# Fused pooled attention and feed-forward kernel: the first batch's loads, transposes and values rearranged, and the first tile's down stage taken by weight piece over four output banks

## The chip, the cores and the metric

One core of one Trainium2 chip runs the whole program. The metric is the device time of one execution in microseconds (us). The kernel before takes 303.81 us (median of 4 executions, 303.62 to 308.21). The span of the trace, from the first to the last instruction, is about 1.8 us shorter than the device time.

## The reference

```python
# q, k, v: (8 batches, 8 heads, 576 positions, 64); w_in (512, 2048); w_out (2048, 512)
k_p = k.reshape(B, H, 72, 8, D).mean(axis=3)          # v_p likewise
attn = softmax(q @ k_p.T / sqrt(D))                   # 576 x 72 per head
x = (attn @ v_p).transpose(0, 2, 1, 3).reshape(4608, 512)
h = x @ w_in
out = (h * cos(h)) @ w_out                            # 4608 x 512, float32
```

## The kernel before

Tokens are worked in nine tiles of 512. A tile has an **up stage** (64 matmuls `x @ w_in` in eight groups; each group fills a pair of PSUM banks, ScalarE takes the cosine of the pair and VectorE multiplies into `g_sb`) and a **down stage** (64 matmuls `g @ w_out`). The attention of the next batch is put between the down matmuls as a list of fills. It is worked in **units**, each a part of a batch's heads and positions: score matmuls, an exp on ScalarE, sums of the exps and their inverse, a **value block** (matmuls of the exps with pooled v) and a VectorE multiply by the inverse into `xT`, the input of the up stage. k and v are pooled by matmuls too. Before tile 0 there is nothing to overlap with, so batch 0's attention is a startup of its own.

The kernel uses eight banks of PSUM, the memory that matmuls write: three pairs (`banks`) and two single output banks (`obanks`). The parts that the change and the argument touch (cut):

```python
banks  = [psum.tile([128, 2, 512], FP32, name=f"bank{i}") for i in range(3)]
obanks = [psum.tile([128, 512], FP32, name=f"obank{i}") for i in range(2)]
msb = ctx.enter_context(tc.tile_pool(name="msb", bufs=3))      # output buffers o_sb: three
...
def up_g(t, fp, between=()):
    h = banks[fp % 3]
    nc.scalar.activation(out=cos, in_=h, func=ACTF.Sin, bias=half_pi[:, :1])
    ...
    nc.vector.tensor_mul(out=g_sb[:, 2 * fp:2 * fp + 2, :], in0=h, in1=cos)

def down_out(t, ms, ps, ...):            # one output chunk: PSUM to o_sb, then two DMAs
    o = msb.tile([128, d_model], FP32, name="o_sb", tag="o_sb")
    nc.vector.tensor_copy(out=o[:, 0:n], in_=ps)
    ...
# startup of batch 0
warm_up(10, obanks[0])                                   # matmuls on constants
pool_k_mm(0, obanks[1], 0, 2)(vec)
warm_up(2, banks[1][:, 0, :])
...                                                      # 9 transposes of q
warm_up(2, banks[1][:, 0, :])
scores(0, us[0], banks[0]); scores(0, us[1], banks[1])   # first exp: time E
...
sums_first(0, us[2], obanks[0])
values_then(0, us[0], obanks[1]); values_then(0, us[1], banks[1][:, 0, :])
sums_first(0, us[3], banks[2][:, 0, :])
values_then(0, us[2], obanks[1]); values_then(0, us[3], obanks[0])
up_mm(0, 0, 0, 2); up_mm(0, 1, 0, 2)                     # first half of 16 up matmuls
...
# tile 0's down stage: two output chunks at a time, batch 1's units between
mms = [(ms, fc) for hm in range(2) for cg in range(4) for ms in range(2 * hm, 2 * hm + 2)
       for fc in range(4 * cg, 4 * cg + 4)]
fill[1:] = [(2, S_(0, 0)), (8, lambda: pool_v_mm(1, banks[1])), ..., (13, V_(0, 1)), ..., (40, V_(3, 0))]
```

Times that the whole text uses, as the prediction names them: **E**, the first exp of batch 0; **R**, when the up matmuls over input chunks 2 and 3 resume (the ninth up matmul); **F**, the first down matmul of tile 0; **T1**, tile 1's first up matmul. The **tail** is T1 to the end of the span. **D** is when TensorE has finished all up-stage work of tile 0 and could start F.

The softmax here doesn't subtract the row's maximum and nothing guards it: scores larger than these inputs give would overflow.

## Time and profile before

| kernel before, profiled execution | us |
|---|---|
| span | 302.1 |
| E / R | 9.25 / 18.98 |
| F (no wait before it) | 33.50 |
| T1 | 53.50 |
| tail | 248.6 |

From T1 on TensorE's up and down matmuls follow each other without gaps in this trace, so the times before T1 are what a change of the startup can move. Besides the lines that the prediction shows, two things will matter later. The first is how TensorE passes the first microseconds (timeline: start, us, engine, line, operation, what is written and read, tile, count):

```profile
1.47 4.45 PE L391 MATMUL obank<-warm 128*128 128x512 bf16 x10 [1.47 <-DVE warm L336]
...
6.84 0.60 PE L391 MATMUL bank<-warm 128*128 128x512 bf16 x2
...
7.78 0.59 PE L391 MATMUL bank<-warm 128*128 128x512 bf16 x2
...
8.80 0.63 PE L211 MATMUL bank<-qT,kk 64*72 64x256 bf16 x8 [0.43 <-DVE qT L193]
```

The first ten matmuls have no use but to keep the array busy; two more follow twice, where TensorE would have waited. Ten take 4.45 us, some 0.43 us for 512 columns. The later pairs take 0.60 and 0.59 us; a matmul's end lies 0.38 us after its start when the clock is full, so their spacing is 0.21 to 0.22 us. The array runs at half speed first and at full speed by 6.84 us; the trace's clock records begin with full clock at 6.51 us.

The second is the load rate in 4 to 6 us (busy time by windows: width of the window, busy us and instructions of PE, its weight loads, VectorE, ScalarE and GpSimd, then granted clock, DMA share and GB/s):

```profile
4.00:6.00 2.00, 2.00 (x11) 0.60 (x11) 1.81 (x3) 1.15 (x1) 1.93 (x5) 1.00 0.97 132
```

The rate counts bytes as they are written. GpSimd's loads turn fp32 into bf16, so 132 GB/s written are 264 GB/s read.

### The profile page before, as it was taken

The numbers are of one execution on the slowest core, as the hardware profiler recorded it, in microseconds if no ns is written. First come the engines' busy times: TensorE is split into PE (matmuls) and PEld (weight loads), VectorE is DVE, ScalarE is ACT, GpSimd is POOL, SyncE is SP. The second block draws the span as 40 slices with busy tenths as digits, with TensorE's granted clock in tenths as the row PEclk, the third lists the DMA queues.
The fourth block names the chain that finished last, engine by engine and source line by source line (L and its number), as shares of the span: only waits on it lengthen the run. The fifth ranks groups of instructions, "written<-read, shape, count | busy, mean of one in ns | idle before, by whom it ended". The sixth has DMA issues, their size and how long they took to land.

```text
span 302.1 us, 4605 instructions
## 1 busy us (share of the span) xinstructions
PE 294.0 (97%) x1798; PEld 141.6 (47%) x1798; DVE 172.3 (57%) x211; ACT 206.8 (68%) x255; POOL 129.8 (43%) x92
## 2 busy tenths in 40 slices
PE   8799999999999999999999999999999999999995
PEld 3545544445544454455444544454444544444444
DVE  5558636574566366645675566656574567425712
ACT  3887897469856986688768876788578956606500
POOL 8553007984973596349733991399100000000000
PEclk9999999999999999999999999999999999999999
DMA  7999999639546943695169617881900330131032
GB/s 152 201 207 206 208 204 196 152 44 174 109 113 105 167 92 70 123 171 113 44 132 161 115 36 162 129 141 36 167 5 1 71 69 0 27 79 35 0 71 71
DMA packets 44006, 32.92 MB, mean 109 GB/s; under 512 B 22096, under 2 KB 39248, under 8 KB 43984
## 3 DMA queue, kind: packets, MB, share of 16 engines
q0 software_dynamic: 19744, 18.07, 38.2%
q1 hardware_dynamic: 24080, 14.42, 21.0%
q8 instruction: 14, 0.23, 0.3%
q10 hardware_dynamic: 160, 0.13, 0.2%
q14 instruction: 8, 0.07, 0.1%
HBM read 36.70 MB, written 9.44 MB: 153 GB/s over the span
## 4 chain that ended last, share of the span: by engine, by line
PE 85%; DMA 10%; POOL 2%; ACT 1%; issue 0%; DVE 0%; POOLq 0%; ACTq 0%
PE obank L310 39%; PE bank L297 37%; DMA w_out_sb<-in_moe_w_out_dram 6%; PE bank L241 5%; DMA w_in_sb<-in_moe_w_in_dram 4%; PE bank L211 3%; PE bank L328 1%; POOL kv_st L84 1%; POOL kp L384 1%; POOL q_b L84 1%; ACT L285 0%; ACT cos L304 0%; ACT ex L218 0%; POOL identity masks.py:197 0%; DVE o_sb L316 0%
## 5 line engine op out<-in xcount | busy, mean ns | idle before, releaser
L310 PE MATMUL obank<-w_out_sb,g_sb 128*128 128x512 bf16 x560 | 132.5, 380 | 0.5 <-DMA w_out_sb<-in_moe_w_out_dram 0.5
L297 PE MATMUL bank<-xT,w_in_sb 128*128 128x512 bf16 x576 | 126.5, 379 | 0.0
L304 ACT ACTIVATE cos<-bank,half_pi 128x1024 f32<-128x1024 f32 x72 | 80.0, 1113 | 63.3 <-PE bank L297 63.3
L307 DVE TENSOR_TENSOR g_sb<-bank,cos 128x1024 bf16<-128x1024 f32 x72 | 88.1, 1225 | 48.2 <-ACT cos L304 48.2
L297 PEld LDWEIGHTS <-w_in_sb 128*128 128x128 bf16 x576 | 55.5, 98 | 68.6 <-DVE xT L252 2.5
L310 PEld LDWEIGHTS <-g_sb 128*128 128x128 bf16 x560 | 52.2, 97 | 56.9 <-issue 3.7
L252 DVE TENSOR_TENSOR xT<-bank,inv 64x512 bf16<-64x512 f32 (+1 forms) x72 | 45.3, 629 | 50.1 <-ACT inv L248 49.2
L141 POOL TENSOR_TENSOR kv_st<-kv_st 72x2048 f32<-72x2048 bf16 x12 | 48.7, 4056 | 35.2 <-DMA kv_st<-in_k_dram 35.2
L247 ACT ACTIVATE lnc<-bank 64x512 f32<-64x512 f32 (+1 forms) x72 | 39.2, 544 | 2.9 <-PE bank L241 1.3
L218 ACT ACTIVATE ex<-bank 72x1024 bf16<-72x1024 f32 (+1 forms) x40 | 35.0, 928 | 5.3 <-PE bank L211 5.2
L316 DVE COPY o_sb<-obank 128x512 f32<-128x512 f32 x35 | 23.6, 689 | 16.8 <-PE obank L310 16.2
L142 POOL TENSOR_TENSOR kv_st<-kv_st 72x1024 f32<-72x1024 f32 x12 | 28.2, 2348 | 1.0
L248 ACT ACTIVATE inv<-lnc 128x512 f32<-128x512 f32 (+1 forms) x36 | 21.0, 583 | 1.1
L241 PE MATMUL bank<-ex,vz 72*128 72x256 bf16 (+1 forms) x176 | 20.0, 243 | 0.2 <-ACT ex L218 0.2
L241 PEld LDWEIGHTS <-vz 72*128 72x128 bf16 x176 | 13.7, 97 | 9.9 <-issue 0.6
L145 POOL TENSOR_TENSOR kp<-kv_st 72x512 bf16<-72x512 f32 x12 | 14.9, 1264 | 0.5
L211 PE MATMUL bank<-qT,kk 64*72 64x256 bf16 (+1 forms) x192 | 13.3, 252 | 1.1 <-ACT qT L193 0.5
L211 PEld LDWEIGHTS <-kk 64*72 64x72 bf16 x192 | 7.6, 110 | 11.9 <-issue 8.1
L285 ACT ACT_TABLE_LOAD x9 | 11.5, 1283 | 0.9 <-PEq L515 0.7
L288 ACT ACT_TABLE_LOAD x9 | 11.5, 1283 | 0.2
L495 POOL COPY gate<-kk 1x1 bf16<-1x1 bf16 x5 | 0.9, 180 | 24.7 <-DMA kk<-kp 24.7
L84 POOL DMA_DIRECT2D q_b<-in_q_dram x10 | 7.7, 773 | 2.7 <-DMA w_in_sb<-in_moe_w_in_dram 1.4
(55 smaller groups left out, 89.8 us busy)
## 6 DMA issues: line engine op xcount, KB each, us to landing
out_dram<-o_sb SPq DMA_DIRECT2D x70, 128.0 KB, 2.4
kv_st<-in_v_dram POOLq DMA_DIRECT2D x8, 576.0 KB, 13.0
kv_st<-in_k_dram POOLq DMA_DIRECT2D x7, 576.0 KB, 7.7
q_b<-in_q_dram POOLq DMA_DIRECT2D x6, 576.0 KB, 9.9
w_in_sb<-in_moe_w_in_dram POOLq DMA_DIRECT2D x4, 512.0 KB, 13.7
w_out_sb<-in_moe_w_out_dram POOLq DMA_DIRECT2D x4, 512.0 KB, 18.4
q_b<-in_q_dram POOLq DMA_DIRECT2D x4, 288.0 KB, 12.1
g_sb<-in_k_dram SPq DMA_DIRECT2D x1, 576.0 KB, 3.5
```

The source lines that it names most:

```text
L141: add(out=s, in0=x[:, :, 0:4, :], in1=x[:, :, 4:8, :], op=ADD)
L142: add(out=s[:, :, 0:2, :], in0=s[:, :, 0:2, :], in1=s[:, :, 2:4, :], op=ADD)
L211: nc.tensor.matmul(pair[:Sp, bank, c:c + n].rearrange("p (g n) -> p g n", n=64), lhsT=kk[b % 2][half[r], h0 + i, 0:Sp], rhs=att["qT", b][h ...
L218: nc.scalar.activation(out=ex[:, 0:nh * n].rearrange("p (a n) -> p a n", a=2), in_=pair[:Sp, :, 0:nh * n // 2], func=ACTF.Exp, scale=scale ...
L241: nc.tensor.matmul(pair[:, hp, (i // 2) * n:(i // 2 + 1) * n], lhsT=vz[b % 2][:, pj, 2 * hp:2 * hp + 2, :].rearrange("p a d -> p (a d)"), ...
L247: nc.scalar.activation(out=lnc[half[1 - hp]], in_=pair[half[1 - hp], hp, 0:w], func=ACTF.Ln)
L252: nc.vector.tensor_mul(out=x_out(b, u, half[hp]), in0=cols(pair[half[hp], hp, :], u), in1=cols(inv[half[1 - hp]], u))
L297: nc.tensor.matmul(h[:, j, :], lhsT=w_in_sb[fc // 4][:, ki, (fc % 4) * 128:(fc % 4 + 1) * 128], rhs=xT[:, ki, t * TILE:(t + 1) * TILE], st ...
L304: nc.scalar.activation(out=cos, in_=h, func=ACTF.Sin, bias=half_pi[:, :1])
L307: nc.vector.tensor_mul(out=g_sb[:, 2 * fp:2 * fp + 2, :], in0=h, in1=cos)
L310: nc.tensor.matmul(o, lhsT=g_sb[:, fc, ms * 128:(ms + 1) * 128], rhs=w_out_sb[fc // 4][:, fc % 4, :], start=(fc == 0), stop=(fc == FFCH - 1))
L316: nc.vector.tensor_copy(out=o[:, 0:n], in_=ps)
```

## The change

It has two parts.

1. **Startup of batch 0.** Half of q comes in fp32 over SyncE's queue behind k's half and is cast on VectorE; v comes in two loads. Pooled k, transposes, sums and values go to other banks, so that ScalarE has one copy less. v is pooled in two halves, the second after the first values; four up matmuls come before the values of units 2 and 3. Seven warm-up matmuls instead of ten, and the two later pairs are gone.
2. **Tile 0's down stage.** The weight pieces are gone through once, each for all four output chunks, so that a late piece of `w_out` is not waited for. Four chunks need four output banks: two halves of pair 2. Batch 1's units then share pairs 0 and 1, and the up groups of tile 0 are rotated by one pair. Batch 1's first pooling of k and its transposes of q run one up group later.

The core of the diff (cut; the new form of `pool_k_mm` and `pool_v_mm` and the moved mask code are left out):

```diff
-    def up_mm ...  h = banks[fp % 3]
+    def h_bank(t, fp):
+        return banks[(fp + (t == 0)) % 3]
...
-    load_even(staged["q", 0], 0, q, 0, 2)
+    for i, (which, src) in enumerate((("k", k), ("q", q))):
+        ...
+        nc.sync.dma_start(out=first[which], in_=even_view(src, 0, 0, 2))
...
-    warm_up(10, obanks[0])
-    pool_k_mm(0, obanks[1], 0, 2)(vec)
-    warm_up(2, banks[1][:, 0, :])
+    warm_up(7, obanks[0])
+    puts = pool_k_mm(0, obanks, 0, 2)
+    cast_first("q", vec)
+    puts[0](act)
+    puts[1](vec)
...
-    warm_up(2, banks[1][:, 0, :])
...
-    pool_v_mm(0, banks[1])
+    pool_v_mm(0, (banks[1][:, 0, :], banks[1][:, 1, :]), 0, 2)
     sums_first(0, us[2], obanks[0])
-    values_then(0, us[0], obanks[1])
-    values_then(0, us[1], banks[1][:, 0, :])
-    sums_first(0, us[3], banks[2][:, 0, :])
-    values_then(0, us[2], obanks[1])
-    values_then(0, us[3], obanks[0])
+    values_then(0, us[0], banks[0][:, 0, :])
+    values_then(0, us[1], banks[0][:, 1, :])
+    pool_v_mm(0, (banks[1][:, 0, :], banks[1][:, 1, :]), 2, 4)
+    sums_first(0, us[3], obanks[1])
     up_mm(0, 0, 0, 2)
+    values_then(0, us[2], obanks[0])
+    values_then(0, us[3], obanks[1])
     up_mm(0, 1, 0, 2)
...
+        ob = [obanks[ms % 2] for ms in range(4)]
         if t == 0:
-            mms = [(ms, fc) for hm in range(2) for cg in range(4) for ms in range(2 * hm, 2 * hm + 2) ...]
+            mms = [(ms, fc) for cg in range(4) for ms in (2, 3, 0, 1) for fc in range(4 * cg, 4 * cg + 4)]
+            ob[2:] = [banks[2][:, i, :] for i in range(2)]
...
-            fill[1:] = [(2, S_(0, 0)), (8, lambda: pool_v_mm(1, banks[1])), ..., (13, V_(0, 1)), ...]
+            fill = [..., (18, S_(1, 0)), (21, V_(0, 1)),
+                    (27, S_(2, 0)), (33, V_(1, 1)), (35, S_(3, 0)), (43, V_(2, 1)), (46, V_(3, 0))]
```

More of the change, by code (lines that the diff above doesn't have):

```diff
@@ L126, in v_part @@
         return vz[b % 2][:, :, 0:4:3, :]
-    def put_kk(b, ps, pj0, pj1, copy):
-        dst = kk[b % 2].rearrange("p (j a) n -> p j a n", a=2)
-        for a in range(2):
-            for r in range(2):
-                copy(out=dst[half[r], pj0:pj1, a, 0:Sp], in_=ps[half[a]])
     def pool_add(b, which):
@@ L148, in pool_add, with pool_k_mm, put, go @@
             add(out=v_part(b), in0=s[..., 0, :], in1=s[..., 1, :], op=ADD)
-    def pool_k_mm(b, bank, pj0, pj1):
+    def pool_k_mm(b, ps, pj0, pj1):
         kb = staged["k", b]
-        ps = bank[:, 0:(pj1 - pj0) * Sp].rearrange("p (j n) -> p j n", n=Sp)
+        ps = [p[half[a], 0:(pj1 - pj0) * Sp].rearrange("p (j n) -> p j n", n=Sp) for a, p in enumerate(ps)]
         for pj in range(pj0, pj1):
             for t in range(ROW):
-                for rows in half:
-                    nc.tensor.matmul(ps[rows, pj - pj0, :], lhsT=kb[rows, pj, t, :], rhs=groups[rows, t, :],
+                for a in range(2):
+                    nc.tensor.matmul(ps[a][:, pj - pj0, :], lhsT=kb[half[a], pj, t, :], rhs=groups[half[a], t, :],
                                      start=(t == 0), stop=(t == ROW - 1))
-        return lambda copy: put_kk(b, ps, pj0, pj1, copy)
-    def pool_v_mm(b, pair):
+        dst = kk[b % 2].rearrange("p (j a) n -> p j a n", a=2)
+        def put(a):
+            def go(copy):
+                for r in range(2):
+                    copy(out=dst[half[r], pj0:pj1, a, 0:Sp], in_=ps[a])
+            return go
+        return put(0), put(1)
+    def pool_v_mm(b, ps, pj0=0, pj1=KCH):
         vb = staged["v", b]
+        ps = [p[:Sp, 0:(pj1 - pj0) * D] for p in ps]
         for t in range(ROW):
             for hp, rows in enumerate(half):
-                nc.tensor.matmul(pair[:Sp, hp, 0:KCH * D], lhsT=groups[rows, t, :], rhs=vb[rows, :, t, :],
+                nc.tensor.matmul(ps[hp], lhsT=groups[rows, t, :], rhs=vb[rows, pj0:pj1, t, :],
                                  start=(t == 0), stop=(t == ROW - 1))
-        nc.vector.tensor_copy(out=v_part(b).rearrange("p j a d -> p a j d"),
-                              in_=pair[:Sp, :, 0:KCH * D].rearrange("p a (j d) -> p a j d", j=KCH))
+        for hp in range(2):
+            nc.vector.tensor_copy(out=v_part(b)[:, pj0:pj1, hp, :], in_=ps[hp].rearrange("p (j d) -> p j d", d=D))
     def k_transpose(b):
@@ L288, in sin_tables @@
         nc.scalar.preload_act_table_set("trig_and_small")
+    def h_bank(t, fp):
+        return banks[(fp + (t == 0)) % 3]
     def up_mm(t, fp, k0=0, k1=KCH):
-        h = banks[fp % 3]
+        h = h_bank(t, fp)
         for j in range(2):
@@ L301, in up_g @@
     def up_g(t, fp, between=()):
-        h = banks[fp % 3]
+        h = h_bank(t, fp)
         cos = msb.tile([128, 2, TILE], FP32, name="cos", tag="cos", bufs=2)
@@ L340, with cast_first @@
     q_tile(0)
-    k_first = g_sb.rearrange("p f n -> p (f n)").bitcast(FP32)[:, 0:2 * ROW * D]
-    nc.sync.dma_start(out=k_first.rearrange("p (j n) -> p j n", j=2), in_=even_view(k, 0, 0, 2))
-    nc.scalar.copy(out=staged["k", 0][:, 0:2].rearrange("p j t d -> p (j t d)"), in_=k_first)
-    load_even(staged["q", 0], 0, q, 0, 2)
+    first = {}
+    for i, (which, src) in enumerate((("k", k), ("q", q))):
+        n = 2 * ROW * D
+        first[which] = g_sb.rearrange("p f n -> p (f n)").bitcast(FP32)[:, i * n:(i + 1) * n].rearrange(
+            "p (j n) -> p j n", j=2)
+        nc.sync.dma_start(out=first[which], in_=even_view(src, 0, 0, 2))
+    def cast_first(which, copy, j0=0, j1=2):
+        copy(out=staged[which, 0][:, j0:j1].rearrange("p j t d -> p j (t d)"), in_=first[which][:, j0:j1])
+    for j in range(2):
+        cast_first("k", nc.scalar.copy, j, j + 1)
     row_of = consts.tile([128, ROW], FP32, name="row_of")
@@ L354 @@
     load_even(staged["q", 0], 0, q, 2, 4)
-    load_even(staged["v", 0], 0, v)
+    load_even(staged["v", 0], 0, v, 0, 2)
+    load_even(staged["v", 0], 0, v, 2, 4)
     identity = consts.tile([128, 128], BF16, name="identity")
@@ L360 @@
     groups = consts.tile([128, ROW, Sp], BF16, name="groups")
-    nc.vector.tensor_tensor(out=dist, in0=row_of.unsqueeze(2).to_broadcast([128, ROW, Sp]),
-                            in1=first_of.unsqueeze(1).to_broadcast([128, ROW, Sp]), op=mybir.AluOpType.subtract)
-    nc.vector.scalar_tensor_tensor(out=sign, in0=dist, scalar=1.0 - POOL, in1=dist, op0=ADD,
-                                   op1=mybir.AluOpType.mult)
-    nc.vector.tensor_scalar(out=groups, in0=sign, scalar1=0.0, scalar2=None, op0=mybir.AluOpType.is_le)
     nc.vector.memset(vz[0], float(POOL))
@@ L371 @@
     nc.vector.memset(half_pi, math.pi / 2.0)
+    nc.vector.tensor_tensor(out=dist, in0=row_of.unsqueeze(2).to_broadcast([128, ROW, Sp]),
+                            in1=first_of.unsqueeze(1).to_broadcast([128, ROW, Sp]), op=mybir.AluOpType.subtract)
+    nc.vector.scalar_tensor_tensor(out=sign, in0=dist, scalar=1.0 - POOL, in1=dist, op0=ADD,
+                                   op1=mybir.AluOpType.mult)
+    nc.vector.tensor_scalar(out=groups, in0=sign, scalar1=0.0, scalar2=None, op0=mybir.AluOpType.is_le)
     kv_even_tiles(1)
@@ L382 @@
     load_even(staged["v", 1], 1, v)
+    nc.gpsimd.memset(vz[1], float(POOL))
     for i in range(2):
@@ L394 @@
     us = BY_HEADS
-    warm_up(10, obanks[0])
-    pool_k_mm(0, obanks[1], 0, 2)(vec)
-    warm_up(2, banks[1][:, 0, :])
-    puts = q_transpose_mm(0, banks[2][:, 0, :], 0, 5), q_transpose_mm(0, obanks[0], 5, 9)
+    warm_up(7, obanks[0])
[3 more added lines that the diff above has]
+    puts[1](vec)
+    puts = q_transpose_mm(0, banks[2][:, 0, :], 0, 5), q_transpose_mm(0, banks[1][:, 0, :], 5, 9)
     puts[0](vec)
     puts[1](act)
-    warm_up(2, banks[1][:, 0, :])
     scores(0, us[0], banks[0])
     scores(0, us[1], banks[1])
-    pool_k_mm(0, obanks[1], 2, 4)(vec)
-    sums_first(0, us[0], banks[0][:, 0, :])
-    puts = q_transpose_mm(0, banks[2][:, 0, :], 9, 14), q_transpose_mm(0, obanks[0], 14, 18)
-    puts[0](vec)
-    puts[1](act)
+    for put in pool_k_mm(0, obanks, 2, 4):
+        put(vec)
+    sums_first(0, us[0], obanks[0])
+    for put in [q_transpose_mm(0, banks[2][:, i, :], 9 + 5 * i, 14 + 4 * i) for i in range(2)]:
+        put(vec)
     sums_first(0, us[1], obanks[1])
@@ L412 @@
     scores(0, us[3], banks[2])
-    nc.vector.memset(vz[1], float(POOL))
-    pool_v_mm(0, banks[1])
+    pool_v_mm(0, (banks[1][:, 0, :], banks[1][:, 1, :]), 0, 2)
     sums_first(0, us[2], obanks[0])
-    values_then(0, us[0], obanks[1])
-    values_then(0, us[1], banks[1][:, 0, :])
-    sums_first(0, us[3], banks[2][:, 0, :])
-    values_then(0, us[2], obanks[1])
-    values_then(0, us[3], obanks[0])
+    values_then(0, us[0], banks[0][:, 0, :])
+    values_then(0, us[1], banks[0][:, 1, :])
+    pool_v_mm(0, (banks[1][:, 0, :], banks[1][:, 1, :]), 2, 4)
+    sums_first(0, us[3], obanks[1])
     up_mm(0, 0, 0, 2)
+    values_then(0, us[2], obanks[0])
+    values_then(0, us[3], obanks[1])
     up_mm(0, 1, 0, 2)
@@ L430 @@
             if t == 0:
-                if fp == 4:
-                    puts = pool_k_mm(1, obanks[0], 0, 2), pool_k_mm(1, obanks[1], 2, 4)
-                elif fp in (5, 6):
-                    g0 = 9 * (fp - 5)
+                if fp == 5:
+                    puts = pool_k_mm(1, obanks, 0, 4)
+                elif fp in (6, 7):
+                    g0 = 9 * (fp - 6)
                     puts = q_transpose_mm(1, obanks[0], g0, g0 + 5), q_transpose_mm(1, obanks[1], g0 + 5, g0 + 9)
-                if fp in (4, 5, 6):
+                if fp in (5, 6, 7):
                     puts[0](vec)
@@ L445 @@
         mms = [(ms, fc) for ms in range(4) for fc in range(FFCH)]
+        ob = [obanks[ms % 2] for ms in range(4)]
         if t == 0:
-            mms = [(ms, fc) for hm in range(2) for cg in range(4) for ms in range(2 * hm, 2 * hm + 2)
-                   for fc in range(4 * cg, 4 * cg + 4)]
+            mms = [(ms, fc) for cg in range(4) for ms in (2, 3, 0, 1) for fc in range(4 * cg, 4 * cg + 4)]
+            ob[2:] = [banks[2][:, i, :] for i in range(2)]
         def S_(n, bank):
@@ L464 @@
         if t == 0:
-            fill[1:] = [(2, S_(0, 0)), (8, lambda: pool_v_mm(1, banks[1])), (8, lambda: values(t, REST, banks[2])),
-                        (11, S_(1, 0)), (13, V_(0, 1)), (18, S_(2, 2)), (21, V_(1, 0, later)), (26, S_(3, 1)),
-                        (32, lambda: later.pop()()), (32, V_(2, 2)), (40, V_(3, 0))]
+            fill = [(2, lambda: scores(t, REST, banks[0])), (2, S_(0, 1)), (10, lambda: values(t, REST, banks[0])),
+                    (11, lambda: pool_v_mm(1, [banks[1][:, i, :] for i in range(2)])), (18, S_(1, 0)), (21, V_(0, 1)),
+                    (27, S_(2, 0)), (33, V_(1, 1)), (35, S_(3, 0)), (43, V_(2, 1)), (46, V_(3, 0))]
         elif b < B:
@@ L487 @@
                 fi += 1
-            down_mm(obanks[ms % 2], ms, fc)
-            if fc == FFCH - 1:
-                down_out(t, ms, obanks[ms % 2])
+            down_mm(ob[ms], ms, fc)
+            if fc == FFCH - 1 and (t, ms) == (0, 3):
+                down_out(t, 2, ob[2])
+            if fc == FFCH - 1 and (t, ms) != (0, 2):
+                down_out(t, ms, ob[ms])
         if t < B:
```

## The prediction

> **What bounds the kernel now.** I read the page first, then the groups by line on the TensorE after 60 us, then the order of time from 0 to 80 us.
>
> ```profile
> PE 294.0 (97%) x1798; PEld 141.6 (47%) x1798; DVE 172.3 (57%) x211; ACT 206.8 (68%) x255; POOL 129.8 (43%) x92
> ```
> ```profile
> L310 PE MATMUL obank<-w_out_sb,g_sb 128*128 128x512 bf16 x496 | 116.8, 379 | 0.0
> L297 PE MATMUL bank<-xT,w_in_sb 128*128 128x512 bf16 x483 | 105.6, 379 | 0.0
> ```
>
> The second fence holds the groups on PE after 60 us (busy, mean ns, idle before): no idle time before either kind of matmul. From tile 1 on the kernel is a gap-free stream on PE. The change edits only batch 0, tile 0 and the fill of batch 1. So the question is one number: when does tile 1's up matmul start? Before, that is 53.50 us, and a shift of it should go through to the end unchanged. The two stretches ahead of it follow, in order of time (start, us, engine, line, what, count, idle before and what ended it).
>
> ```profile
> 8.80 0.63 PE L211 MATMUL bank<-qT,kk 64*72 64x256 bf16 x8 [0.43 <-DVE qT L193]
> ...
> 9.25 1.93 ACT L218 ACTIVATE ex<-bank 72x1024 bf16<-72x1024 f32 x2 [0.68 <-PE bank L211]
> ...
> 12.23 0.57 ACT L193 COPY qT<-obank 128x512 bf16<-128x512 bf16 x1
> ...
> 17.13 8.96 PE L297 MATMUL bank<-xT,w_in_sb 128*128 128x512 bf16 x40
> ...
> 18.24 0.69 DVE L282 TENSOR_TENSOR xT<-obank,inv 128x512 bf16<-128x512 f32 x1 [0.50 <-ACT inv L271]
> ```
>
> ScalarE works without pause from 9.25 (first exp) to 18.2 us; the last multiply into xT ends at 18.93 and the up matmuls over chunks 2 and 3 resume at once (18.99). Call the first exp E and the resumption R: R = E + 9.74.
>
> ```profile
> 31.27 0.67 PE L192 MATMUL obank<-identity,q_b 128*128 128x128 bf16 x9
> 31.47 1.11 ACT L304 ACTIVATE cos<-bank,half_pi 128x1024 f32<-128x1024 f32 x1 [0.64 <-PE bank L297]
> ...
> 32.62 1.23 DVE L307 TENSOR_TENSOR g_sb<-bank,cos 128x1024 bf16<-128x1024 f32 x1 [0.38 <-ACT cos L304]
> ...
> 34.84 1.23 DVE L307 TENSOR_TENSOR g_sb<-bank,cos 128x1024 bf16<-128x1024 f32 x1 [1.00 <-ACT cos L304]
> ...
> 36.12 1.17 PE L165 MATMUL bank<-kv_st,groups 64*72 64x256 bf16 x18
> ...
> 38.10 0.81 PE L310 MATMUL obank<-w_out_sb,g_sb 128*128 128x512 bf16 x3 [0.46 <-DMA w_out_sb<-in_moe_w_out_dram]
> ...
> 39.62 0.60 PE L241 MATMUL bank<-ex,vz 72*128 72x256 bf16 x4
> ...
> 42.22 1.39 DVE L252 TENSOR_TENSOR xT<-bank,inv 64x512 bf16<-64x512 f32 x2 [2.44 <-ACT inv L248]
> ...
> 47.87 0.61 PE L241 MATMUL bank<-ex,vz 72*128 72x256 bf16 x4
> ```
>
> Three things are to be seen. A bank pair that an up matmul filled is free 2.58 us after its last matmul (31.27 to 32.62 + 1.23 = 33.85). The pooling of v (36.12) goes into the last up pair and starts 0.05 us after that pair's multiply ends (34.84 + 1.23 = 36.07). A unit's values hold their pair from 39.62 to 42.22 + 1.39 = 43.61, 3.99 us. The only DMA wait is for the second piece of w_out (38.10): about 0.55 us, as PE could have gone on at 37.55.
>
> **What the skill says.** "PSUM — Partial Sum Buffer", section "PSUM bank collisions raise a hardware error", has PSUM guarded by bank, so a matmul into a pair waits until its readers are done; the 0.05 us above agrees. "DMA: Bandwidth & Descriptors", section "Issuing engines are not separate DMA queues", says that loads of any issuing engine run on the same 16 DMA engines, so SyncE's queue adds no bandwidth: the trace moves fp32 at 392 GB/s written when k's half is alone, and 207 GB/s of bf16 (twice that read) with GpSimd's queue full. "VectorE: DVE Perf Modes", section "The perf-mode tier table", gives 1227 ns for an fp32 copy of 2048 elements in SBUF; scaled, the cast of 1152 is an estimated 0.69 us. Nothing before shows it. "TensorE: Matmul & The Clock Gate", Part 1, has the array at half clock until about 3.4 us of sustained work; the trace grants full clock at 6.5 us, after ten warm-up matmuls from 1.47 us.
>
> **Part 1, q's half.** q's half queues behind k's on SyncE: k's packets run to 3.95 us and k lands at 4.28. Alone, q's half would take 1.5 us more and land near 5.8; sharing with GpSimd's queue, which starts at 3.7 us and ramps, it lands nearer 6.5 to 7 (7.05 before). Then the cast (0.7), 0.6 for two pooled-k copies behind it on VectorE (0.3 each in the trace), 0.5 for a transpose copy: scores 1.4 after the cast, exp 0.45 after that (8.80 to 9.25). E = 6.5 + 0.7 + 1.4 + 0.45 = 9.05 to 9.1, between 8.3 and 10.1. I take -0.1 us.
>
> **Part 2, ScalarE and the last units of batch 0.** One copy leaves ScalarE (12.23, 0.57), but the first sums now share an output bank with the pooled k, whose copies end about 0.25 us later than the sums were wanted; exp 3 ends at E + 6.45 instead of E + 6.52. VectorE then has two multiplies (about E + 6.2 to 7.5) and, in program order after them, the two copies of v's second half (about 0.5). The first up matmul now goes into the pair that these copies read: it starts near E + 8.05. Four up matmuls (0.86) come before the values of units 2 and 3, whose multiplies need 0.1 + 0.5 + 2 x 0.69 more. R = E + 8.05 + 0.86 + 0.1 + 0.5 + 1.38 = E + 10.9, against E + 9.74: +1.15 us. The first w_in piece (16.75) is in by then; removing one GpSimd load ahead of it makes it earlier if anything.
>
> **Part 3, up stage.** The same 56 matmuls, pooling and transposes: 14.5 us from R to the first down matmul (18.99 to 33.50), no change. w_in's last piece (landed 28.71) is wanted after 40 of them and the pooling, near 29.5 or later, so it still is in time.
>
> **Part 4, down stage.** Its work without waits: 64 matmuls at 0.216 (64 take 13.98 in one row of the trace, less one 0.38 end, over 63) are 13.8; four score blocks 0.44 (38.10 + 3 x 0.216 = 38.75 to 39.18), four value blocks 0.44 (39.62 to 40.06), the rest of batch 0 0.35 + 0.3, pooling v 1.2: 19.2 us. Before: 20.0, with 0.55 and 0.2 in waits. By weight piece, 16 matmuls stand before each new piece, so the w_out wait goes: -0.55. But:
> - In tile 0 the up pairs are rotated by one, so the last pair is pair 2, and the first down matmul (output chunk 2) goes into pair 2. Transposes take 0.5 of the 2.58 + 0.05 that the pair is held: PE stands 2.1 us.
> - Batch 1's units have two pairs. Counting from that matmul (F): values 0 at F + 7.3 free pair 1 at 11.3, values 1 are due at 10.7: 0.55. Values 1 free it at 15.3, values 2 are due at 14.35: 0.95.
> - Values 3 start at 16.4; behind values 2 on ScalarE, they leave pair 0 at 21.1, when tile 1's first up matmul is due at 20.7: 0.4.
>
> Down stage: 19.2 + 2.1 + 0.55 + 0.95 + 0.4 = 23.2 to 23.3, +3.25 us.
>
> **Sum.** -0.1 + 1.15 + 3.25 = +4.3 us: 303.87 + 4.3 = 308.2.
>
> **Rivals.**
> 1. *The w_out wait was the bound and going through the pieces once pays.* For: it is in the chain of waits, with 18.43 us of DMA before 38.10. Against: PE stood only 0.55 us. If the pair waits of part 4 did not exist, 303.87 - 0.55 - 0.2 + about 1 = 304.1; with an early E, 303.
> 2. *q's half lands near 5.8 and everything moves up by 0.8 us.* For: GpSimd's queue moves little between 3.7 and 5 us, so there is room. Against: part 4 hangs on F and not on E. Time 307.4.
> 3. *The clock stays at half longer,* as seven warm-ups end at 4.5 us and PE then waits for the cast and the mask. For: less than 3.4 us of sustained work. Against: the pooling of k at about 5 us continues it. Transposes and scores slow down by 0.5 us, at worst some of the up stage by 1.7: 308.7 to 309.9.
> 4. *VectorE's cast runs at single rate* (1.2 us): +0.5, 308.7.
>
> **Range and chances.** Part 4's first wait comes from durations that repeat to 0.02 us; the two-pair waits could be off by 0.4 each, E by 0.8, R by 0.4. Together about +-1.3, and a little more at the bottom for something that I placed on the path and is not: 306.2 to 309.8. 2% below is 297.8, which no part reaches (all idle time of PE before 53.50 that the change touches is smaller): 0.01. 2% above is 309.95: 0.08.
>
> **What would show it.** Right: in the chain of waits or the waits list, PE's first L310-type matmul of tile 0 waiting some 2 us for VectorE's multiply into g_sb; two waits of PE's values for VectorE's xT of 0.5 to 1 us in the same stage; no wait for w_out; tile 1's up matmul at 57 to 58.5 us; the first exp near 9.1 us. Wrong: the first down matmul within 0.6 us of the last transpose, or E below 8.2 us, or a time below 305; that would mean that the bank waits don't stand on PE's path as I read them.

## The result, and the profile after

The changed kernel is correct and takes **315.67 us** (median of 4: 313.57, 315.60, 315.74, 316.32) against 303.81. The ratio is 1.0384 (95% interval 1.0333 to 1.0435): slower. Ratios here are the mean time of one kernel's fast runs over that of the other's of the same rounds, so they are not quite the ratio of the medians quoted. Executions over 1.5% slower than the fastest of the same kernel are left out of the means. The predicted range ended at 309.8; even the fastest execution lies 3.8 us above it. The trace is of that fastest execution.

| profiled execution | before | after | difference |
|---|---|---|---|
| E | 9.25 | 9.07 | -0.18 |
| R | 18.98 | 24.50 | +5.52 |
| R to D | 14.52 | 14.52 | 0.00 |
| D to T1 | 20.00 | 23.11 | +3.11 |
| tail | 248.6 | 249.67 | +1.07 |
| span | 302.1 | 311.8 | +9.7 |

(D is 33.50 before, where F has no wait, and 39.02 after: the last transpose starts at 38.96, and one takes 0.06 us.) The page's first part, which lists busy time, shares and instruction counts, hides nearly all of this; TensorE's share falls by one point:

```profile
PE 299.4 (96%) x1809; PEld 144.6 (46%) x1809; DVE 171.3 (55%) x212; ACT 207.0 (66%) x255; POOL 130.8 (42%) x93
```

TensorE did some of the same work more slowly, and slow work counts as busy. The stream of later tiles is as it was (groups on TensorE after 70 us: busy us and mean ns of one, then idle before):

```profile
L318 PE MATMUL obank<-w_out_sb,g_sb 128*128 128x512 bf16 x496 | 116.8, 379 | 0.0
L305 PE MATMUL bank<-xT,w_in_sb 128*128 128x512 bf16 x482 | 105.4, 379 | 0.0
```

**The startup** (timeline of after, the lines that answer to those of before):

```profile
1.47 3.17 PE L410 MATMUL obank<-warm 128*128 128x512 bf16 x7 [1.47 <-DVE warm L344]
...
5.82 0.76 DVE L358 CAST q_b<-g_sb 128x1152 bf16<-128x1152 f32 x1 [1.04 <-DMA g_sb<-in_q_dram]
...
7.93 1.52 PE L216 MATMUL bank<-qT,kk 64*72 64x256 bf16 x8 [0.16 <-DVE qT L198]
...
9.07 1.93 ACT L223 ACTIVATE ex<-bank 72x1024 bf16<-72x1024 f32 x2 [0.67 <-PE bank L216]
...
18.17 0.64 PE L285 MATMUL bank<-ex,vz 72*64 72x256 bf16 x4 [0.85 <-DVE xT L287]
...
20.49 1.87 PE L305 MATMUL bank<-xT,w_in_sb 128*128 128x512 bf16 x4
...
23.29 8.96 PE L305 MATMUL bank<-xT,w_in_sb 128*128 128x512 bf16 x39
```

R is the fifth matmul of the last line, at 24.50. Compare the eight score matmuls: 1.52 us here, 0.63 us before. And the first four up matmuls at 20.49 us take 1.87 us, which is a spacing of 0.43 us, as of the first warm-ups. So TensorE is still at half clock at 22 us; the trace's clock records begin with full clock only at 24.01 us. The page's row of granted clock reads 9 (tenths) from the start in both kernels, as there is no record before the first grant. **For the startup the spacing of matmuls has to be read, not that row.** The line at 18.17 shows a second thing: the values of unit 1 wait 0.85 us for VectorE's multiply, which reads the values of unit 0 in the other half of the same pair.

The loads did better than the prediction's best guess. q's half is there for the cast at 5.82 us (7.05 before), and the windows view of after has for 4 to 6 us:

```profile
4.00:6.00 2.00, 1.49 (x30) 0.85 (x30) 0.93 (x3) 1.25 (x2) 1.93 (x5) 1.00 1.10 316
```

These are 316 GB/s written where there were 132. The gain is smaller than it looks, as SyncE's load stays fp32: the DMA view of 4 to 6 us has 0.50 MB written by SyncE's queue and 0.13 MB by GpSimd's, before 0.26 MB, all by GpSimd's. With GpSimd's bytes doubled, 0.76 MB were read for 0.52, half as much again: SyncE's queue filled a stretch in which GpSimd's had not reached the 207 GB/s that it writes later. But E moved by 0.18 us only: the cast takes 0.76 us, and transposes and scores run at half clock.

**The down stage and the start of tile 1:**

```profile
39.86 1.23 DVE L315 TENSOR_TENSOR g_sb<-bank,cos 128x1024 bf16<-128x1024 f32 x1 [0.38 <-ACT cos L312]
...
41.14 0.59 PE L318 MATMUL bank<-w_out_sb,g_sb 128*128 128x512 bf16 x2 [1.96 <-DVE g_sb L315]
...
52.17 0.61 PE L246 MATMUL bank<-ex,vz 72*128 72x256 bf16 x4 [0.39 <-DVE xT L257]
...
56.20 0.61 PE L246 MATMUL bank<-ex,vz 72*128 72x256 bf16 x4 [0.82 <-DVE xT L257]
...
62.13 5.35 PE L305 MATMUL bank<-xT,w_in_sb 128*128 128x512 bf16 x24 [0.34 <-DVE xT L257]
...
66.56 0.69 DVE L324 COPY o_sb<-obank 128x512 f32<-128x512 f32 x1 [2.58 <-DMA out_dram<-o_sb]
...
68.44 3.83 PE L305 MATMUL bank<-xT,w_in_sb 128*128 128x512 bf16 x17 [0.96 <-DVE g_sb L315]
```

The first down matmul waits 1.96 us until VectorE's multiply (39.86 + 1.23 = 41.09) has read pair 2; two value blocks wait for their pair; no wait for `w_out` is left. An idle time here begins at a matmul's end, 0.38 us after its start, though the next could have followed after 0.22 us. Counted from the starts, the four waits (the last is that of T1) cost 2.12, 0.55, 0.98 and 0.50 us. The last two lines are the part of the tail that grew. Four output chunks now end close together, there are three `o_sb` buffers, and the fourth copy waits 2.58 us for an output DMA. VectorE does tile 1's multiplies after that copy, from 67.17 us on, and TensorE's third up group waits for its pair (0.96 us of idle time; the starts of the two matmuls are 1.34 us apart).

### The profile page after: what moved, and what is told of

It is laid out like the page before. It is cut to its first block, busy times and chain, and to the rows that moved or that the text cites. A ratio compares the mean times of both kernels' runs of the same rounds, so it can differ in the third digit from the quotient of the medians.

```text
span 311.8 us, 4634 instructions
## 1 busy us (share of the span) xinstructions
PE 299.4 (96%) x1809; PEld 144.6 (46%) x1809; DVE 171.3 (55%) x212; ACT 207.0 (66%) x255; POOL 130.8 (42%) x93
## 2 busy tenths in 40 slices
DMA packets 44022, 33.21 MB, mean 107 GB/s; under 512 B 22112, under 2 KB 39008, under 8 KB 44000
## 4 chain that ended last, share of the span: by engine, by line
PE 87%; ACT 5%; DVE 3%; DMA 2%; issue 1%; SPq 0%; ACTq 0%; DVEq 0%
PE bank L305 39%; PE obank L318 35%; PE bank L246 5%; PE bank L216 3%; ACT lnc L252 2%; DMA g_sb<-in_q_dram 1%; DVE xT L257 1%; PE bank L336 1%; PE bank L318 1%; DMA out_dram<-o_sb 1%; ACT inv L253 1%; PE obank L152 1%; DVE g_sb L315 1%; ACT ex L223 1%; ACT cos L312 1%; PE bank L197 1%
## 5 line engine op out<-in xcount | busy, mean ns | idle before, releaser
L318 PE MATMUL obank<-w_out_sb,g_sb 128*128 128x512 bf16 x528 | 125.2, 379 | 0.0
L324 DVE COPY o_sb<-obank 128x512 f32<-128x512 f32 x33 | 22.2, 689 | 16.8 <-PE obank L318 13.6
L216 PE MATMUL bank<-qT,kk 64*72 64x256 bf16 (+1 forms) x192 | 14.3, 262 | 0.3 <-DVE qT L198 0.2
L103 POOL DMA_DIRECT2D kv_st<-in_v_dram x6 | 5.0, 842 | 17.3 <-PE bank L170 17.3
```

The lines of the kernel that those rows point to most:

```text
L216: nc.tensor.matmul(pair[:Sp, bank, c:c + n].rearrange("p (g n) -> p g n", n=64), lhsT=kk[b % 2][half[r], h0 + i, 0:Sp], rhs=att["qT", b][h ...
L318: nc.tensor.matmul(o, lhsT=g_sb[:, fc, ms * 128:(ms + 1) * 128], rhs=w_out_sb[fc // 4][:, fc % 4, :], start=(fc == 0), stop=(fc == FFCH - 1))
```

## The experiments

The main theory was that three things add up: half clock in the startup, the order of units in the startup, and the bank waits of the down stage. The main rival was that the new order of work alone explains R and the clock only follows it. The table holds all runs; the times E to T1 are those of one execution, the profiled one. The runs were made on three chips, each with the kernel before beside them, and the ratio is to that. "Clock" is the stretch at full clock up to 60 us.

| run | median, range | ratio [95%] | E | R | F | T1 | tail | clock |
|---|---|---|---|---|---|---|---|---|
| a1_warm | 312.15 (310.46-313.47) | 1.0296 [1.0273, 1.0319] | 8.59 | 22.06 | 38.70 | 59.69 | 249.0 | 4.54-14.78, and from 21.60 |
| b1_cold | 305.04 (303.56-305.89) | 1.0042 [1.0006, 1.0078] | 9.17 | 21.63 | 36.18 | 55.56 | 248.55 | 4.62-8.04, 14.87-18.28, and from 21.69 |
| b2_loads | 302.84 (302.74-303.26) | 0.9978 [0.9963, 0.9992] | 8.93 | 18.67 | 33.19 | 52.56 | 248.51 | from 5.07 |
| b3_down | 310.01 (309.11-310.94) | 1.0211 [1.0184, 1.0239] | 9.36 | 19.09 | 36.23 | 58.88 | 250.28 | half in 37.47-40.88 |
| a4_hold | 309.00 (308.41-311.04) | 1.0184 [1.0156, 1.0213] | 9.04 | 20.57 | 37.22 | 58.22 | 249.01 | from 6.52 |
| b4_osb4 | 308.51 (307.86-313.26) | 1.0149 [1.0129, 1.0169] | 8.99 | 18.95 | 36.09 | 58.66 | 248.67 | half in 36.54-39.95 |
| b5_order | 305.91 (305.54-309.91) | 1.0100 [1.0052, 1.0149] | 8.78 | 18.69 | 33.21 | 55.10 | 248.66 | from 5.41 |
| b6_best | 303.10 (302.74-304.84) | 0.9992 [0.9972, 1.0013] | 8.73 | 18.48 | 33.00 | 52.37 | 248.59 | held |
| a6_values | 310.62 (309.95-310.93) | 1.0206 [1.0149, 1.0263] | 9.15 | 19.90 | 36.54 | 59.16 | 249.49 | half in 37.48-40.90 |
| a7_repaired | 306.05 (305.89-306.34) | 1.0059 [1.0012, 1.0105] | 8.44 | 19.38 | 34.41 | 55.73 | 248.53 | from 4.49 |
| b7_fill | 303.00 (302.92-303.16) | 0.9958 [0.9921, 0.9995] | 8.47 | 18.57 | 33.09 | 52.65 | 248.52 | held |
| b8_loads5 | 303.02 (302.78-303.11) | 0.9956 [0.9919, 0.9993] | 8.94 | 18.68 | 33.19 | 52.80 | 248.50 | held |

All were correct. Names with a start from the changed kernel, names with b from the kernel before. The one slow execution in the table (b4_osb4, 313.26) is in its range and not in its ratio. The ratios of the four runs from a6_values on are some 0.1% low and their intervals wide: one execution of the kernel before there took 307.41 us and counts. Without it b8_loads5 and b7_fill are at 0.997.

### a1_warm: the changed kernel with the warm-ups of before

```diff
-    warm_up(7, obanks[0])
+    warm_up(10, obanks[0])
     puts = pool_k_mm(0, obanks, 0, 2)
+    warm_up(2, banks[0][:, 0, :])
     cast_first("q", vec)
...                                   # and warm_up(2, ...) again after the transposes
```

> The changed kernel with the warm-up matmuls of before put back: ten at the start, two after the first pooling of k, two after the first transposes of q. Theory A (the array stays at half clock because the change took seven warm-ups out): full clock from about 6.5 us and held, the first exp at 8.3 to 8.7 us instead of 9.07, the up matmuls over chunks 2 and 3 (R) at E + 10.9, so 19.2 to 19.6 us instead of 24.5, and 303.8 + 0.4 (R) + 3.1 (down stage) + 1.1 (tile 1) = 308.0 to 308.8 us, with executions within 1 us of each other. Theory B (R is late because of the new order of work on VectorE and TensorE, whatever the clock): R stays beyond 23 us and the time at 313 us or above.

It took 312.15 us, 3.5 us less than the changed kernel, and R came at 22.06 instead of 24.50. The full clock was granted at 4.54 us and **taken back** at 14.78, though the longest idle gap of TensorE in the 3.4 us before that was 0.93 us (timeline of a1_warm):

```profile
14.21 0.41 PE L271 MATMUL obank<-ex,ones 72*64 72x256 bf16 x4 [0.93 <-ACT ex L223]
...
18.02 1.87 PE L305 MATMUL bank<-xT,w_in_sb 128*128 128x512 bf16 x4
```

Four sums take 0.41 us here and the next four, at 17.36, 0.64 us; the four up matmuls have the half-clock 1.87 us again. Neither expectation held as it stands: E is as theory A has it, but R and the time lie between the two. So the removed warm-ups were a part of the loss, and the new order loses the clock even with them.

### b1_cold: the kernel before with the warm-ups of after

```diff
-    warm_up(10, obanks[0])
+    warm_up(7, obanks[0])
     pool_k_mm(0, obanks[1], 0, 2)(vec)
-    warm_up(2, banks[1][:, 0, :])
...                                   # the second warm_up(2, ...) removed too
```

> The kernel of before with seven warm-ups in place of ten and without the two pairs later; nothing else changed. Theory A: the clock is granted late or taken back, R moves from 18.99 to 20 us or later, the time is 306 to 311 us and differs between executions by more than 1 us. Theory B: the warm-ups that are left are enough, 303.8 us as before.

R rose from 18.98 to 21.63 (E + 12.46 instead of E + 9.74) with nothing changed but dummy matmuls, so in this execution the clock alone costs the kernel before 2.7 us up to R (timeline of b1_cold; the kernel before has 0.63 us in place of the 1.28):

```profile
8.28 1.28 PE L211 MATMUL bank<-qT,kk 64*72 64x256 bf16 x8 [0.40 <-DVE qT L193]
```

T1 rose by only 2.06, as the later down stage has no wait for `w_out`: F to T1 is 19.38 us for 20.00. The traced execution is the slowest: they spread from 303.56 (mean clock 0.994) to 305.89 (0.983), and the median is 1.4 us above that of before on this chip, less than the 306 to 311 expected.

### b2_loads and b8_loads5: the kernel before with the loads of after

```diff
-    load_even(staged["q", 0], 0, q, 0, 2)
+    nc.sync.dma_start(out=first["q"], in_=even_view(q, 0, 0, 2))   # fp32, behind k's half
-    load_even(staged["v", 0], 0, v)
+    load_even(staged["v", 0], 0, v, 0, 2)
+    load_even(staged["v", 0], 0, v, 2, 4)
...
+    cast_first("q", vec)                                            # ahead of the pooled-k copies
```

> The kernel of before (all its warm-ups) with the load part of the change alone: q's half in fp32 over SyncE's queue and its cast on VectorE, v in two loads, the mask after the memsets. Theory A (loads are what the change does well): q's half lands at 5.8 us, w_in's first piece at 15.4 instead of 16.75 and w_out's second at 36.8 instead of 38.06, the first exp at 8.9 (the four copies of pooled k wait behind the cast), no wait for w_out: 303.8 - 0.35 - 0.5 = 302.8 to 303.1 us. Rival: the transfer was hidden, 303.8.

It is a little faster: 0.9978, with an interval below 1, and T1 at 52.56 (53.50 before). No wait for `w_out` is left in its trace: R is 0.31 us earlier, and F to T1 takes 19.37 us for 20.00. So the wait that the new down stage was made to remove goes with the loads alone. The same kernel with five rounds:

> The kernel of b2_loads once more, beside b7_fill on one chip with five rounds, as the difference to before is a third of a per cent: 302.7 to 302.9 us, a ratio of 0.997 with an interval that leaves out 1.

This gave 0.9956, all six executions within 302.78 to 303.11. The load part (with it go k's cast in two pieces and the mask code behind the memsets, which no run takes apart) is worth 0.8 us or so: T1 moved by 0.94 and 0.70 in the two traces.

### b3_down: the kernel before with the down stage of after

```diff
-        h = banks[fp % 3]
+        h = h_bank(t, fp)
...                                   # order of chunks 2, 3, 0, 1 and four output banks, as in the change
-            fill[1:] = [(2, S_(0, 0)), ...]
+            fill = [(2, lambda: scores(t, REST, banks[0])), (2, S_(0, 1)), ...]
```

> The kernel of before with the down part of the change alone: rotated up pairs in tile 0, matmuls by weight piece over four output banks, batch 1's units on two pairs. Theory A: PE waits 2.1 us for the last up pair, 0.4 + 0.8 us for two values blocks, 0.4 at the end, and another 1.1 us in tile 1, where the fourth output copy waits for one of three output buffers: 303.8 + 3.1 + 1.1 = 307.6 to 308.3 us. Rival: without the half clock these waits do not stand on the path and the w_out wait of 0.55 goes: 303.2.

R is that of before (19.09). R to T1 takes 39.79 us against 34.52, and the tail is 1.7 us longer; 310.01 us are more than the 307.6 to 308.3 expected. The first two lines show that the wait for pair 2 has a second price, the last two the late output copy of the tail (timeline of b3_down):

```profile
36.23 0.59 PE L313 MATMUL bank<-w_out_sb,g_sb 128*128 128x512 bf16 x2 [2.46 <-DVE g_sb L310]
...
37.24 2.55 PE L313 MATMUL bank<-w_out_sb,g_sb 128*128 128x512 bf16 x6
...
63.91 0.69 DVE L319 COPY o_sb<-obank 128x512 f32<-128x512 f32 x1 [3.16 <-DMA out_dram<-o_sb]
...
65.78 4.48 PE L300 MATMUL bank<-xT,w_in_sb 128*128 128x512 bf16 x20 [1.54 <-DVE g_sb L310]
```

The wait is 2.46 us here (no transposes lie behind the last up group). The six matmuls after it have a spacing of 0.43 us: full clock was taken back at 37.47 and came again at 40.88, 3.41 us later. In two other executions of this kernel the mean clock was 1.0 and the time 309.11 and 309.38; in the two with 0.994 it was 310.64 and 310.94. That is some 1.5 us for one such stretch.

### b4_osb4: b3_down with four output buffers

```diff
-        o = msb.tile([128, d_model], FP32, name="o_sb", tag="o_sb")
+        o = msb.tile([128, d_model], FP32, name="o_sb", tag="o_sb", bufs=4)
```

> The run b3_down with four output buffers in place of three. Theory: the fourth output copy no longer waits for an output transfer, so tile 1's stall of 1.5 us goes and the time from tile 1's first up matmul to the end is 248.6 us instead of 250.3: 310.0 - 1.5 = 308.3 to 308.8. Rival (the third up pair of tile 1 is late for another reason, such as the two output copies that read it): no change, 310.

The tail fell from 250.28 to 248.67, that of before, and the late wait of tile 1's third up group (1.54 us in b3_down) was gone. Three buffers for four bunched outputs are the cause of the longer tail.

### b5_order: b4_osb4 with the output chunks in the order 0, 1, 2, 3

```diff
-            mms = [(ms, fc) for cg in range(4) for ms in (2, 3, 0, 1) for fc in range(4 * cg, 4 * cg + 4)]
+            mms = [(ms, fc) for cg in range(4) for ms in range(4) for fc in range(4 * cg, 4 * cg + 4)]
```

> The run b4_osb4 with the output chunks in the order 0, 1, 2, 3 in place of 2, 3, 0, 1, so that the last up pair is wanted after eight matmuls and not at once. Theory: the first down matmul starts within 0.3 us of the last up matmul's end, the stall of 2.6 us and the half-clock window after it go, the two-pair waits of 0.5 + 1.0 and the one at the end of 0.5 stay: 304.6 to 305.6 us. Rival (the wait for the pair only moves to the ninth matmul): 307.5 or more.

Chunks 0 and 1 go to the single output banks, which are free, so TensorE has eight down matmuls of work before it needs pair 2. F came at 33.21 with no wait, the clock stayed full in the traced execution, and R to T1 fell from 39.71 to 36.41, of which up to 1.7 us are the half-clock stretch in b4_osb4's trace. The medians differ by 2.6 us. One of the four executions took 309.91 us at a mean clock of 0.981; its trace was not kept:

```profile
33.21 0.59 PE L313 MATMUL obank<-w_out_sb,g_sb 128*128 128x512 bf16 x2
...
34.22 1.47 PE L313 MATMUL obank<-w_out_sb,g_sb 128*128 128x512 bf16 x6
```

What remains against before is 1.89 us from R to T1. TensorE's largest waits in it are those of two value blocks for their pair (1.2 us together) and 0.3 us each of T1 for a pair and of v's pooling for an exp.

### a4_hold: a1_warm with ten dummy matmuls in three gaps

```diff
     for put in pool_k_mm(0, obanks, 2, 4):
         put(vec)
+    warm_up(3, banks[2][:, 0, :])
...
+    warm_up(4, obanks[0])            # before the sums of unit 2
...
+    warm_up(3, obanks[1])            # before the values of unit 1
```

> The run a1_warm plus ten dummy matmuls in three places of batch 0 where its TensorE stood idle (three before the first sums, four before the third sums, three between the first two values blocks), in output banks that are free there. In a1_warm's trace the clock was granted at 4.5 us, taken back at 14.8 and granted again at 21.6. Theory A (thin windows lose the clock, and the half clock is what R has beyond the order of work): no half clock after the first grant, R at E + 11.9 (10.9 of the prediction and 1.05 because the second values block waits for the first one's multiply), so about 20.5 us instead of 22.1, and 308.6 to 309.6 us with executions within 1 us. Rival (the fillers only add work, the clock is not it): 312 us as a1_warm or more.

The clock was held from 6.52 us on, and R came at 20.57 = E + 11.53, in a kernel that does all the work of the changed one and 17 dummy matmuls more. After's R is 3.93 later with an E that differs by 0.03: that is the half clock, separated from the order of work. The time is as expected, the spread is not: one execution took 311.04 us at a mean clock of 0.992. The line to compare with the 1.87 us of after and a1_warm:

```profile
17.76 1.02 PE L305 MATMUL bank<-xT,w_in_sb 128*128 128x512 bf16 x4 [0.24 <-DVE vz L173]
```

### a6_values: a4_hold with the second value block in another pair and v pooled at once

```diff
-    pool_v_mm(0, (banks[1][:, 0, :], banks[1][:, 1, :]), 0, 2)
-    warm_up(4, obanks[0])
+    pool_v_mm(0, (banks[1][:, 0, :], banks[1][:, 1, :]))
+    warm_up(3, obanks[0])
...
-    warm_up(3, obanks[1])
-    values_then(0, us[1], banks[0][:, 1, :])
-    pool_v_mm(0, (banks[1][:, 0, :], banks[1][:, 1, :]), 2, 4)
+    values_then(0, us[1], banks[1][:, 0, :])
```

> The run a4_hold with v of batch 0 pooled at once, ahead of the third sums, and the second values block in another pair (1) than the first (0). Theory: of the 1.8 us by which the new order makes R late at full clock, 0.85 is the second values block waiting for the first one's multiply, as both write halves of one pair, and the rest mostly v's second copies between the multiplies and the first up matmul; with both gone R is at E + 10.6, 0.9 us earlier than in a4_hold, and the time 307.9 to 308.4 us. Rival: the values of units 2 and 3 behind four up matmuls are what makes R late, no change beyond 0.2 us (308.8 to 309).

It has four dummy matmuls fewer than a4_hold. R moved as it should, to E + 10.75, and the 0.85-us wait was gone. The time did not: 310.62 is 1.6 us more than a4_hold (on another chip). The down stage's wait for pair 2 was the same (1.96 us), but in this execution full clock was taken back at 37.48 for 3.42 us, and all four executions had a mean clock of 0.992, where three of a4_hold's four had 0.999 or 1.0. The likely reason is that the startup had moved and the same wait fell differently against the clock's period; the runs do not show that by themselves. The expectation on the time missed by the half-clock stretch and, in the two traces, by a tail that is 0.5 us longer.

### a7_repaired: a6_values with the two repairs of the down stage

```diff
+        o = msb.tile([128, d_model], FP32, name="o_sb", tag="o_sb", bufs=4)
+            mms = [(ms, fc) for cg in range(4) for ms in range(4) for fc in range(4 * cg, 4 * cg + 4)]
```

> The run a6_values with four output buffers and the output chunks in the order 0, 1, 2, 3: every cause found taken out of the changed kernel except the two pairs for batch 1's units. Theory: minus 1.6 (first down matmul waits 0.5 instead of 2.1 us) and minus 0.45 (tile 1): 305.8 to 306.5 us, so still about 2 us over before, which are the waits on two pairs in the down stage (0.5 + 1.0 + 0.5). Rival: a cause is still missing, 307.5 or more.

It took 306.05 us, all executions within 305.89 to 306.34 at a clock of 0.998 to 1.0. So 9.6 of the 11.9 us that the change cost (medians) are undone by four repairs that leave its plan as it is: dummy matmuls, another bank for one value block with v pooled in one piece, one more output buffer, another order of chunks. TensorE's waits (us in total, times, longest) show what is left in the down stage:

```profile
PE bank L246 <- DVE xT L257: 1.2, 2, 0.8
PE obank L318 <- DVE qT L198: 0.4, 1, 0.4
PE bank L305 <- DVE xT L257: 0.3, 1, 0.3
PE bank L170 <- ACT ex L223: 0.3, 1, 0.3
```

The wait for pair 2 is not among them; the two value blocks on two pairs are, and the down stage now waits a little for the copy of a transpose that sits in an output bank.

### b6_best and b7_fill: what is the best that these parts give

```diff
# b6_best: b2_loads with
-    put_k = pool_k_mm(0, obanks[1], 0, 2)
+    put_k = pool_k_mm2(0, obanks, 0, 2)     # the pooled k in two banks: one copied by ScalarE, one by VectorE
...                                          # transposes 5 to 9 to banks[1], warm-ups to banks[0]
# b7_fill: b6_best with
+    warm_up(1, banks[2][:, 0, :])           # after the second half of pooled k
+    warm_up(2, obanks[0])                   # before the sums of unit 2
+    warm_up(1, banks[0][:, 1, :])           # before the values of unit 2
```

> The run b2_loads with the first pooling of k in two output banks, as in the change, so that ScalarE copies one half while VectorE casts q and copies the other. Theory: the first exp at 8.3 to 8.5 us instead of 8.93, and everything on TensorE up to 0.5 us earlier unless w_out's second piece (36.8 us) becomes the wait: 302.3 to 302.7 us. Rival: w_out's landing holds tile 0's down matmuls and nothing is gained: 302.84.

> The run b6_best with four dummy matmuls in three gaps of batch 0. b6_best's executions lay between 302.7 and 304.8 us, the longer ones at a mean clock of 0.994. Theory: thin windows lose the clock there too in some executions; with the gaps filled no execution is above 303.2, median 302.5 to 302.8 us. Rival: no change of median and spread.

b6_best gained nothing over b2_loads that the intervals show (0.9992, up to 1.0013): its profiled T1 is 0.19 earlier, but two of its executions had a clock of 0.994 and took 303.76 and 304.84. b7_fill, with four dummy matmuls more, has T1 0.28 later than b6_best and the smallest spread of all, 0.24 us; its median of 303.00 is a little above the 302.5 to 302.8 expected. **b2_loads / b8_loads5 and b7_fill are faster than the kernel before by 0.2 to 0.4%**, about 0.8 us of 303.8. They share the load part, with q's half over SyncE's queue; the down stage of the change is in none of them.

## Why the prediction was wrong

The prediction added -0.1 (E), +1.15 (R), 0 (up stage), +3.25 (down stage) and 0 (tail). The profiled execution gave -0.18, +5.52 - (-0.18) = +5.70, 0.00, +3.11 and +1.07. Point by point:

**Right: the question and the sign.** From 70 us on the stream of matmuls is as dense as before, and nearly all of the time is decided ahead of it. The change costs more than it saves.

**Right: part 4, the down stage.** D to T1 is 23.11 where 23.2 to 23.3 was worked out. The wait for pair 2 was put at 2.1, the waits on two pairs at 0.55, 0.95 and 0.4, and the `w_out` wait at zero; counted from the starts they are 2.12, 0.55, 0.98 and 0.50, and no `w_out` wait. Durations read from the trace and program order were enough for that. b5_order confirms the first wait from the other side, and the two-pair waits stay in a7_repaired.

**Right: parts 1 and 3.** E was put at 9.05 to 9.1 and is 9.07, though by errors that cancel: q landed 0.7 us or more earlier than "nearer 6.5 to 7", the cast took 0.76 instead of 0.7, and transposes and scores ran at half clock. Rival 2 had q's landing right (5.8) and its effect wrong, because the change also took away the clock. b2_loads, which keeps the clock, has E at 8.93 and T1 0.94 earlier; b7_fill has E at 8.47.

**Wrong: part 2, "R = E + 10.9".** It came at E + 15.43. The sum was made of durations at full clock. At full clock (a4_hold) it is E + 11.53, so the order of work was 0.63 short. The miss lies ahead of the first up matmul, which was put at E + 8.05 and came at E + 8.72; from there to R are 2.81 us, as worked out (2.84). Most of that is the second value block, which the prediction let run at once: in after and a1_warm it waits 0.85 us for the multiply that reads the first block in the other half of the pair, and in a6_values, where it has another pair, R is E + 10.75. But a6_values also pools v at once, so the 0.78 between a4_hold and a6_values is not the bank alone.

**Wrong: rival 3, as sized.** The prediction did name the half clock, and gave it 0.5 us with "at worst some of the up stage by 1.7". It cost 3.9 us up to R in the fastest execution. The step that failed is the sentence "The pooling of k at about 5 us continues it": after seven warm-ups it did not bring the clock, and nothing up to 20.6 us did. The grant came only at 24.01 us, behind a stretch of up matmuls.

How activity sets the clock can be read in part. The changes of clock lie at multiples of 3.41 us from each other: a1_warm from 4.54 to 14.78 (3 x 3.41) and to 21.60 (2 more), b3_down from 37.47 to 40.88. If one lays windows of 3.41 us on these edges and takes 0.216 us per 512 columns (0.43 at half clock) as the time in which the array streams, matmuls that overlap counted once, full clock followed in these traces on windows with 0.87 and more streaming (after has 0.60, 0.68, 0.77, 0.57, 0.88 and 0.57 at half clock, then 0.92 and the grant). It was lost behind windows with 0.23 to 0.55. This is my own working, and it gives no clean limit: after's 0.88 brought no grant, and windows with 0.37 to 0.49 in other traces kept the clock. The edges lie elsewhere in each trace (the first grant comes at 4.5 to 6.8 us in the runs with all warm-ups), so a wait of 2 us falls into one window or into two. That fits the spread of executions of one kernel, but was not tested by itself.

**Wrong: "a shift of it should go through to the end unchanged".** The tail grew by 1.07 us. The prediction counted banks and did not count `o_sb` buffers. b4_osb4 shows the cause: one buffer more and the tail is that of before.

**The sum of the miss.** In the profiled execution, against +4.3: half clock +3.9, order of units +0.6, tail +1.1, down stage -0.1, E -0.1; together +5.4, and 4.3 + 5.4 = 9.7 us, the whole difference. The median is another 2.1 us higher. The other executions had mean clocks of 0.967, 0.982, 0.993 and 0.967 (a fifth, 315.78 us) against 0.998 for the traced one. More half clock is likely, but the mean does not follow the time (the slowest, 316.32, has 0.993), as it leaves out what comes before the first grant. Their traces were not kept, and where they lost time is open.

## What to carry to other kernels

In a startup, judge an edit by how dense TensorE's work stays as well as by its waits: matmuls that look useless may hold the clock, and a wait can cost more than its length in the matmuls behind it. Before you give a stage its first output bank, ask who reads that bank last; the order of four chunks was worth 2.6 us here. When outputs bunch, count the buffers behind them too. And try the parts of a change one by one: the loads alone gained what the new order of the down stage was made for.

## What the Trainium skill lacked or had wrong

- "TensorE: Matmul & The Clock Gate", section "HAM oscillation — how this bites in real kernels": it gives as the rule that TensorE must have no idle gap over about 3.4 us (the page's next section does have short idle times making the clock swing, without a measure). Here full clock was lost with no gap over 0.93 us (a1_warm, at 14.78 us) and behind single waits of 1.96 and 2.46 us (a6_values, b3_down), while 1.96 us did not cost it in a4_hold's trace. The changes of clock 3.41 us apart agree with the page's period; the length of one gap as the measure does not. How full a window has to be to gain or to keep the clock is what the page lacks; in these traces every grant followed a window of 0.87 and more, one such window brought none, and there is no clean limit for the loss.
- "DMA: Bandwidth & Descriptors", section "Issuing engines are not separate DMA queues": it says that issuing from several engines saves only the issuing time. Here q's half came 1.26 us earlier over SyncE's queue (5.79 for 7.05 us) and the first `w_in` piece 1.33 us earlier (15.42 for 16.75), more than the 0.87 us that GpSimd took to issue q's half. In 4 to 6 us 0.76 MB were read where there had been 0.52. The page elsewhere gives GpSimd's path the slower setup, which fits. Whether that slow start or the conversion to bf16 held the load before, no run tells.
- No page has what a mean granted clock leaves out: in the changed kernel's traced execution it reads 0.998, though matmuls run at half speed up to 24.01 us, because the records begin with the first grant.
- No page has that work on the two halves of a pair declared as one buffer can wait for each other: 0.85 us for the second value block. Whether it is the program's tracking or the chip that asks for it, no run tells.
